# A product of the MLP backward pass, made in the output passes and reloaded from DRAM for the w2 gradient

## The chip, the cores and the metric

The kernel runs on one core of a Trainium2 chip. The core has a matrix engine (TensorE, PE in the profile, with its weight loads as PEld), a vector engine (VectorE, DVE), an engine for activations (ScalarE, ACT), a general-purpose engine (GpSimd, POOL) and a queue engine (SyncE, SP) that issues transfers. POOL issues transfers too, among them the gathers and scatters by index. Every engine works through its own list of instructions in order; semaphores make one wait for another. Sixteen DMA engines move the bytes of all queues. The metric is the device time of one execution in microseconds (us); less is better.

## What is computed

One block of a network, its output and the gradients of nine of its inputs, for 2048 tokens of width D = 1024 and an MLP of width F = 3584, in bf16. A row of modulation values (sa, ca, ga, sb, cb, gb) comes from a vector c. The forward pass, without its helpers:

```
mod = (silu(c) @ w_mod).reshape(1, 6, 1, -1)
sa, ca, ga, sb, cb, gb = (mod[:, k] for k in range(6))
h = layernorm(x) * (1 + ca) + sa
x = x + ga * A(h, w_r, w_i)
h = layernorm(x) * (1 + cb) + sb
x = x + gb * B(h, w1, b1, w2, b2)
...
out, vjp = jax.vjp(f, A_x, A_w_r, A_w_i, B_w1, B_b1, B_w2, B_b2, c, w_mod)
grads = vjp(grad_out)
```

A is a filter in the two-dimensional Fourier domain. B normalises its input, multiplies by w1, adds b1, applies gelu, multiplies by w2 and adds b2. The change concerns one intermediate of the backward pass, gB = grad_out * gb, a 2048 x 1024 array that is the gradient at the output of B. The gradient of w2 is the transposed hidden layer times gB.

## The kernel before

The tokens are cut into 16 groups of 128 (one per partition of the on-chip memory) and handled in four chunks of four groups, b = 0 to 3. A chunk doesn't hold four neighbouring groups: in it groups 0 and 3 are plain rows of the tensor, and groups 1 and 2 are rows in reversed order, an order that the Fourier stage wants. An input is therefore loaded into a chunk by `load_tok` (L126) with three transfers: one plain load on SP for groups 0 and 3 (L128), and two gathers by index on POOL (L131). `load_tok_half` (L135) does the same for one half h of the columns (L137 and L142); `store_tok_half` writes a chunk back with one plain store on SP (L155) and two scatters on POOL (L160). Intermediates that the kernel keeps in DRAM for itself (d_x1, d_n3, d_A and others) are stored in chunk order, so that one plain transfer moves a whole chunk (`chunk_rows`, L120).

The work goes through these stages, all in one program:

- the modulation rows, a product ph of grad_out * gb with the transposed w2 (L659), and the forward Fourier stage;
- the MLP stage, about 380 to 780 us of the span. It has 28 blocks (`z_block`, L762) that compute the hidden layer of one seventh of F for one chunk (L776) and its gelu and derivative on ScalarE and VectorE, and eight output passes (`bo_pass`, L803), one for each chunk b and column half h, here named (b,h). A pass multiplies the hidden layer by w2 in seven steps g = 0 to 6 (L817), each with a block of w2 loaded by SP into one of four slots (w2sA to w2sD, L812). After the seventh step it loads half a chunk of x1 into x1t (L822) and of grad_out into go (L823), copies the sums out of PSUM on ScalarE into bo (L826), forms go * bo, bo * gb and bo + x1t on VectorE (L827 to L829), and stores the result. Two steps into the next pass, TensorE sums the columns of go * bo in four matmuls `pa` (L836). The three parts bo, x1t and go belong to one tile, `otile`, of which there is one. A list `plan` (L853) fixes how blocks and steps follow one another; in pass (3,0) and (3,1) no blocks are left;
- the stage that multiplies by the transposed w1 (L996) and goes back through the second layer norm, chunk by chunk;
- the gradient of w2 (`gw2_mm`, L1089, matmuls at L1090). Before it, L1034 to L1041 make the four chunks of gB: `load_tok` from grad_out, then one multiply by the gb row on VectorE. The tiles gB0 to gB3 lie in the buffers px2 to px5, which until then hold the first four blocks of the transposed w1 (w1T). The hidden layer comes in through transposing loads on SP (`hh_load`, L1115), of which all but the first are issued after the last load of gB (L1174);
- the backward Fourier stage, in which pieces of the w2 and w1 gradients (`fill`) are laid between other work, and the w1 gradient (L1157).

The framework orders the instructions of each engine ahead of time by a priority, which is the place in the program unless `tc.high_priority()` raises it, and by a model of when each is ready; `tc.issue_after(x)` puts an instruction behind x on its engine. It inserts the waits on semaphores, also those of a buffer that is written while an earlier user still reads it. The order is thus not the program's: loads are often issued well ahead of their place in it.

Of the kernel before, what the change touches and what calls it, by code (L numbers as in the profile page):

```python
# [11 lines left out]
BF16 = mybir.dt.bfloat16  # L12
I32 = mybir.dt.int32
ACT = mybir.ActivationFunctionType
ALU = mybir.AluOpType
# [3 lines left out]
S = 2048  # L19
D = 1024  # L20
# [15 lines left out]
def kernel(  # L36
# [24 lines left out]
    nc = tc.nc  # L61
# [5 lines left out]
    dram = ctx.enter_context(tc.tile_pool(name="dram", bufs=1, space=bass.MemoryType.DRAM))  # L67
# [26 lines left out]
    opca_row, ga_row, opcb_row, gb_row = (rows4[:, r, :] for r in range(4))  # L94
# [9 lines left out]
    d_x1 = dram.tile([S, D], BF16, name="d_x1")  # L104
    d_A = dram.tile([S, D], BF16, name="d_A")
    d_n3 = dram.tile([S, D], BF16, name="d_n3")
    d_gx1 = dram.tile([S, D], BF16, name="d_gx1")
    d_ph = dram.tile([F, S], BF16, name="d_ph")
    d_hh = dram.tile([F, S], BF16, name="d_hh")
    d_gz = dram.tile([F, S], BF16, name="d_gz")  # L110
# [9 lines left out]
    def chunk_rows(dt, i):  # L120
        return dt[4 * i * P:4 * (i + 1) * P, :].rearrange("(q p) d -> p q d", p=P)

    def tok_flat(ap):
        return ap[0] if len(ap.shape) == 3 else ap

    def load_tok(t4, src, i, eng=None):  # L126
        s3 = tok_flat(src)
        ins = (eng or nc.sync).dma_start(out=t4[:, 0:4:3, :],  # L128
                          in_=bass.AP(tensor=s3.tensor, offset=s3.offset + 128 * i * D, ap=[[D, P], [1024 * D, 2], [1, D]]))
        for q in range(2):  # L130
            nc.gpsimd.indirect_dma_start(out=t4[:, 1 + q, :], out_offset=None, in_=s3,  # L131
                                         in_offset=bass.IndirectOffsetOnAxis(ap=xidx[:, 2 * i + q:2 * i + q + 1], axis=0))
        return ins

    def load_tok_half(t4, src, i, h):  # L135
        s3 = tok_flat(src)
        nc.sync.dma_start(out=t4[:, 0:4:3, :],  # L137
                          in_=bass.AP(tensor=s3.tensor, offset=s3.offset + 128 * i * D + h * KH, ap=[[D, P], [1024 * D, 2], [1, KH]]))
        s2 = s3.rearrange("n (h d) -> (n h) d", h=2)
        for q in range(2):  # L140
            k = 4 * i + 2 * q + h
            nc.gpsimd.indirect_dma_start(out=t4[:, 1 + q, :], out_offset=None, in_=s2,  # L142
                                         in_offset=bass.IndirectOffsetOnAxis(ap=oidx[:, k:k + 1], axis=0))
# [9 lines left out]
    def store_tok_half(dst, t4, i, h):  # L153
        s3 = tok_flat(dst)
        nc.sync.dma_start(out=bass.AP(tensor=s3.tensor, offset=s3.offset + 128 * i * D + h * KH, ap=[[D, P], [1024 * D, 2], [1, KH]]),  # L155
                          in_=t4[:, 0:4:3, :])
        s2 = s3.rearrange("n (h d) -> (n h) d", h=2)
        for q in range(2):
            k = 4 * i + 2 * q + h
            nc.gpsimd.indirect_dma_start(out=s2, out_offset=bass.IndirectOffsetOnAxis(ap=oidx[:, k:k + 1], axis=0),  # L160
                                         in_=t4[:, 1 + q, :], in_offset=None)
# [7 lines left out]
    def bcn(row, n):  # L169
        return bass.AP(tensor=row.tensor, offset=row.offset, ap=[row.ap[0], [0, n], row.ap[1]])  # L170

    def tt(out, a, b, op):
        return nc.vector.tensor_tensor(out=out, in0=a, in1=b, op=op)  # L173
# [476 lines left out]
    def ordered():  # L650
        return tc.issue_after(last_pe[0].ins)
# [93 lines left out]
    otile = []  # L745
# [57 lines left out]
    def bo_pass(b, h):  # L803
        cs_ = slice(h * KH, (h + 1) * KH)
        pbs = [(ps_f if b < NB - 1 or h == 0 else (ps_s, ps_d)[k % 2])("pbo") for k in range(4)]
        for i in range(4):
            with ordered():
                last_pe[0] = nc.tensor.matmul(pbs[i][:], lhsT=ones_bf[0:1, :], rhs=b2_row[0:1, cs_], start=True, stop=False)
        for g in range(7):
            wp = w2p[w2n[0] % 4]  # L810
            w2n[0] += 1
            nc.sync.dma_start(out=wp, in_=w2_v[:, g * 4:(g + 1) * 4, cs_])  # L812
            hh = hh_slots[(b * 7 + g) % 11]
            for i in range(4):
                for k in range(4):
                    with ordered():
                        last_pe[0] = nc.tensor.matmul(pbs[i][:], lhsT=hh[:, k, i * P:(i + 1) * P], rhs=wp[:, k, :],  # L817
                                                      start=False, stop=(g == 6 and k == 3))
            if g < 6:
                yield  # L820
        bo, x1t, go = (otile[0][:, k] for k in range(3))
        nc.sync.dma_start(out=x1t, in_=chunk_rows(d_x1, b)[:, :, cs_])  # L822
        load_tok_half(go, grad_out, b, h)  # L823
        for i in range(4):
            with tc.high_priority():
                last_ev[0] = nc.scalar.copy(out=bo[:, i, :], in_=pbs[i][:])  # L826
        tt(go, go, bo, ALU.mult)  # L827
        tt(bo, bo, bcn(gb_row[:, cs_], 4), ALU.mult)
        tt(bo, bo, x1t, ALU.add)  # L829
        store_tok_half(out_0, bo, b, h)  # L830

        yield
        pa = (ps_d if b < NB - 1 else ps_f)("pa")
        for i in range(4):
            with ordered():
                last_pe[0] = nc.tensor.matmul(pa[:], lhsT=ones_bf[:], rhs=go[:, i, :], start=(i == 0), stop=(i == 3))  # L836
        with tc.high_priority():
            if b == 0:
                nc.vector.tensor_copy(out=gacc[:, cs_], in_=pa[0:1, :])  # L839
            else:  # L840
                tt(gacc[:, cs_], gacc[:, cs_], pa[0:1, :], ALU.add)

    def bo_both(b):
        for h in range(2):
            late = bo_pass(b, h)
            for _ in range(7):
                next(late)
                yield
            bo_late.append(late)
# [116 lines left out]
    fold2_in = {}  # L966
# [67 lines left out]
    gBs = []  # L1034
    for b in range(NB):
        gb_t = reg.tile([P, 4, D], BF16, name=f"gB{b}", tag=PXT[2 + b])
        gb_in = load_tok(gb_t, grad_out, b)
        with tc.high_priority():
            with tc.issue_after(fold2_in[2].ins):
                tt(gb_t[:], gb_t[:], bcn(gb_row, 4), ALU.mult)  # L1040
        gBs.append(gb_t)  # L1041
    smA2 = reg.tile([P, 2, 4, 512], BF16, name="smA2", tag="sma")
    smB2 = reg.tile([P, 2, 4, 512], BF16, name="smB2", tag="smb")
# [213 lines left out]
```

## Time and profile before

| | us |
|---|---|
| runs: median (lowest, highest) of 3 | 1522.13 (1520.72, 1531.21) |
| span of the profiled execution | 1521.4 |
| VectorE multiplies of gB, 4 of 128x4096 | 2.29 each |
| VectorE multiplies of otile by a row, 8 of 128x2048 | 1.22 each |
| gathers of gB on POOL, 8: issue; to landing | 0.95 to 1.97; 10.3 to 13.2 |
| gathers of go on POOL, 16: issue; to landing (median) | 0.97 to 1.68; 5.0 |
| loads of x1t on SP, 8: to landing (median) | 5.7 |
| stores of d_gz on POOL, 28: issue; to landing (median, longest) | 0.75; 4.7; 9.9 |
| transposing loads hht on SP, 8: to landing (median) | 7.1 |

The profile is of one execution. Its span runs from the first to the last instruction; the times of the runs were measured without it. Times in views count from the start of the span. L173 is the line of the helper for element-wise operations, so those are told apart by their tiles; `rows` is the tile that holds the gb row.

### The profile page before, as it was taken

What the parts mean: (1) busy time and instruction counts of PE and PEld (TensorE: products, weight loads), DVE (VectorE), ACT (ScalarE), POOL (GpSimd) and SP (SyncE); (2) the same over time, 40 slices, a digit from 0 to 9 for tenths busy, and PEclk for the clock granted to TensorE, in tenths of its full rate; (3) what the DMA queues carried; (4) which work ended last, traced back from release to release, by engine and by line L of the source; (5) the groups of instructions that cost most, each with busy time, mean ns of one, the idle gap of its engine ahead of it and who ended that gap; (6) DMA issues with size and microseconds to landing.
All of it is one profiled execution on the core that took longest, in us unless ns stands there. A gap on an engine that the chain in (4) does not pass through costs nothing.

```text
span 1521.4 us, 18355 instructions
## 1 busy us (share of the span) xinstructions
PE 1437.8 (95%) x6831; PEld 667.6 (44%) x6831; DVE 1072.0 (70%) x1577; ACT 722.1 (47%) x956; POOL 363.5 (24%) x428
## 2 busy tenths in 40 slices
PE   5889899999999999999989999979998899999998
PEld 2434445444444444444334444434444444444443
DVE  5992868897799887877224977967066666898633
ACT  4765556668876666655012333322522344443211
POOL 5720621111112122220210101311033421322423
PEclk8999999999999999999999999989999999999999
DMA  9972745989587876999956336496288986766996
GB/s 327 282 207 66 198 150 176 280 258 339 193 265 238 211 254 216 257 282 271 322 170 205 135 101 221 109 275 176 63 201 225 235 242 183 197 174 163 257 206 195
DMA packets 358160, 324.27 MB, mean 213 GB/s; under 512 B 209187, under 2 KB 300849, under 8 KB 357816
## 3 DMA queue, kind: packets, MB, share of 16 engines
q1 hardware_dynamic: 324184, 207.71, 52.4%
q0 software_dynamic: 33888, 115.41, 22.5%
q8 instruction: 53, 0.87, 0.2%
q14 instruction: 35, 0.29, 0.1%
HBM read 164.15 MB, written 109.10 MB: 180 GB/s over the span
## 4 chain that ended last, share of the span: by engine, by line
PE 47%; DVE 22%; DMA 10%; issue 10%; ACT 6%; POOL 3%; SPq 1%; POOLq 0%; ACTq 0%; DVEq 0%
PE pbo L817 11%; PE pz L776 9%; PE gw2acc L1090 8%; PE pg L996 5%; DVE ct L173 4%; PE pv L544 3%; PE pu L451 3%; PE gw1acc L1157 2%; PE pp L659 2%; DVE got L895 2%; DVE fbuf L173 1%; DMA gB<-in_grad_out_dram 1%; DVE gn3a L900 1%; DMA out_dram<-otl 1%; DVE gt L173 1%
## 5 line engine op out<-in xcount | busy, mean ns | idle before, releaser
L659 PE MATMUL pp<-gBoT,wt 128*128 128x512 bf16 x896 | 200.4, 379 | 1.9 <-ACT pho L669 1.0
L1157 PE MATMUL gw1acc<-gzh,n3n 128*128 128x512 bf16 x896 | 197.0, 380 | 0.3 <-DMA gzh<-d_gz 0.3
L996 PE MATMUL pg<-w1T,gzr 128*128 128x512 bf16 x896 | 196.3, 380 | 0.4
L776 PEld LDWEIGHTS <-w 128*128 128x128 bf16 x896 | 87.7, 98 | 109.0 <-issue 3.8
L996 PEld LDWEIGHTS <-gzr 128*128 128x128 bf16 x896 | 88.0, 98 | 107.5 <-issue 2.9
L1157 PEld LDWEIGHTS <-n3n 128*128 128x128 bf16 x896 | 87.8, 98 | 104.3 <-issue 0.6
L659 PEld LDWEIGHTS <-wt 128*128 128x128 bf16 x896 | 87.4, 98 | 103.0 <-DMA wt<-in_B_w_dram 1.4
L776 PE MATMUL pz<-n3Tb,w 128*128 128x512 bf16 x448 | 99.1, 379 | 1.5 <-DVE w2sD L839 1.5
L1090 PE MATMUL gw2acc<-gB,hhsA 128*128 128x512 bf16 x448 | 100.1, 379 | 0.0
L776 PE MATMUL pz<-n3Ta,w 128*128 128x512 bf16 x448 | 98.7, 379 | 1.3 <-ACT gt L779 1.3
L817 PEld LDWEIGHTS <-hhA 128*128 128x128 bf16 x608 | 59.9, 99 | 79.0 <-issue 10.8
L1095 ACT CAST gwo<-gw2acc 128x512 bf16<-128x512 f32 x54 | 30.6, 584 | 122.4 <-PE gw2acc L1090 80.1
L779 ACT ACTIVATE gt<-pz,b_col 128x512 bf16<-128x512 f32 x112 | 72.9, 684 | 29.5 <-PE pz L776 29.0
L785 ACT ACTIVATE gt<-gt 128x2048 bf16<-128x2048 bf16 x28 | 53.4, 1910 | 64.4 <-DVE gt L173 64.4
L173 DVE TENSOR_TENSOR gt<-gt,gt 128x2048 bf16<-128x2048 bf16 x56 | 68.5, 1224 | 15.9 <-ACT gt L787 15.1
L1161 ACT CAST gwo<-gw1acc 128x512 bf16<-128x512 f32 x48 | 27.7, 584 | 109.1 <-PE gw1acc L1157 87.5
L173 DVE TENSOR_TENSOR ct<-ct 128x2048 bf16<-128x2048 bf16 x64 | 76.0, 1219 | 0.8
L1090 PE MATMUL gw2acc<-gB,hht 128*128 128x512 bf16 x256 | 58.9, 392 | 8.7 <-DVE gB L173 8.4
L1090 PEld LDWEIGHTS <-hhsA 128*128 128x128 bf16 x448 | 43.8, 98 | 50.4
L781 ACT ACTIVATE gt<-gt 128x2048 bf16<-128x2048 bf16 x28 | 53.5, 1910 | 7.6 <-DVE gb_acc L796 6.9
L787 ACT ACTIVATE gt<-gt 128x2048 bf16<-128x2048 bf16 x28 | 53.3, 1909 | 0.4
L1162 POOL DMA_DIRECT2D out_dram<-gwo x56 | 30.7, 551 | 77.9 <-ACT gwo L1161 38.3
(314 smaller groups left out, 2552.9 us busy)
## 6 DMA issues: line engine op xcount, KB each, us to landing
gzr<-d_gz SPq DMA_DIRECT2D x28, 512.0 KB, 7.7
wblk<-in_w_mod_dram SPq DMA_DIRECT2D x12, 1024.0 KB, 13.4
d_ph<-pho POOLq DMA_DIRECT2D x21, 512.0 KB, 5.2
out_dram<-otl POOLq DMA_DIRECT2D x40, 256.0 KB, 3.7
d_hh<-hhA POOLq DMA_DIRECT2D x19, 512.0 KB, 4.8
w2sD<-in_B_w_dram SPq DMA_DIRECT2D x14, 512.0 KB, 6.1
hhC<-d_ph SPq DMA_DIRECT2D x14, 512.0 KB, 5.1
w2sA<-d_ph SPq DMA_DIRECT2D x14, 512.0 KB, 4.0
```

The costliest lines, as they stand in the source:

```text
L173: return nc.vector.tensor_tensor(out=out, in0=a, in1=b, op=op)
L451: last_pu[0] = nc.tensor.matmul(pu[:], lhsT=fb[:, i, cl, c8 * P:(c8 + 1) * P], rhs=sm[:, i, :], start=(i == 0), stop=(i == 3))
L659: last_pe[0] = nc.tensor.matmul(pp[:], lhsT=wt[:, fg % 2, cch, k * P:(k + 1) * P], rhs=gBoT[j][:, cch, :], start=(cch == 0), stop=(cch == ...
L776: last_pe[0] = nc.tensor.matmul(pz[:], lhsT=w1s[g][:, cch, k * P:(k + 1) * P], rhs=n3T[:, cch, :], start=(cch == 0), stop=(cch == NDC - 1))
L779: nc.scalar.activation(out=zb[:, k, :], in_=pz[:], func=ACT.Identity, bias=b1_col[:, fc:fc + 1], scale=1.0)
L781: nc.scalar.activation(out=av, in_=zb, func=ACT.Square)
L785: nc.scalar.activation(out=sg, in_=bv, func=ACT.Sigmoid, scale=2.0 * GK)
L787: nc.scalar.activation(out=bv, in_=bv, func=ACT.Sigmoid, scale=-2.0 * GK)
L817: last_pe[0] = nc.tensor.matmul(pbs[i][:], lhsT=hh[:, k, i * P:(i + 1) * P], rhs=wp[:, k, :], start=False, stop=(g == 6 and k == 3))
L996: nc.tensor.matmul(pgs[i][:], lhsT=gzt[g][:, k, i * P:(i + 1) * P], rhs=w1Ts[g][:, k, h * KH:(h + 1) * KH], start=(g == 0 and k == 0), sto ...
L1090: nc.tensor.matmul(acc[:], lhsT=hh_s[hh_o[fc]][:, t, :], rhs=gBs[t // 4][:, t % 4, h * KH:(h + 1) * KH], start=(t == 0), stop=(t == NT - 1))
L1157: nc.tensor.matmul(acc[:], lhsT=n3ns[t // 4][:, t % 4, cch * P:(cch + 1) * P], rhs=gz2[t // 8][:, t % 8, :], start=(t == 0), stop=(t == NT ...
```

## The change

gB is made in the output passes. After step g = 2 of each pass the half chunk of grad_out is loaded into go, multiplied by the gb row into x1t, and x1t is stored by POOL to a new DRAM tensor d_gB in chunk order; then x1t is loaded from d_x1. Both loads stood after step 6 before. Ahead of the w2 gradient each gB tile is loaded from d_gB by one plain load on SP, without gathers and without a multiply.

```diff
+    d_gB = dram.tile([S, D], BF16, name="d_gB")
...
             for i in range(4):
                 for k in range(4):
                     with ordered():
                         last_pe[0] = nc.tensor.matmul(pbs[i][:], lhsT=hh[:, k, i * P:(i + 1) * P], rhs=wp[:, k, :],
                                                       start=False, stop=(g == 6 and k == 3))
+            if g == 2:
+                bo, x1t, go = (otile[0][:, k] for k in range(3))
+                load_tok_half(go, grad_out, b, h)
+                tt(x1t, go, bcn(gb_row[:, cs_], 4), ALU.mult)
+                nc.gpsimd.dma_start(out=chunk_rows(d_gB, b)[:, :, cs_], in_=x1t)
+                nc.sync.dma_start(out=x1t, in_=chunk_rows(d_x1, b)[:, :, cs_])
             if g < 6:
                 yield
-        bo, x1t, go = (otile[0][:, k] for k in range(3))
-        nc.sync.dma_start(out=x1t, in_=chunk_rows(d_x1, b)[:, :, cs_])
-        load_tok_half(go, grad_out, b, h)
...
     for b in range(NB):
         gb_t = reg.tile([P, 4, D], BF16, name=f"gB{b}", tag=PXT[2 + b])
-        gb_in = load_tok(gb_t, grad_out, b)
-        with tc.high_priority():
-            with tc.issue_after(fold2_in[2].ins):
-                tt(gb_t[:], gb_t[:], bcn(gb_row, 4), ALU.mult)
+        gb_in = nc.sync.dma_start(out=gb_t[:], in_=chunk_rows(d_gB, b))
         gBs.append(gb_t)
```

## The prediction

> **What bounds the kernel now.** The page's first part and its chain come first: TensorE is busy for 95% of the span and carries 47% of the chain, and one load of this change, gB from grad_out, stands in that chain by name.
>
> ```profile
> PE 1437.8 (95%) x6831; PEld 667.6 (44%) x6831; DVE 1072.0 (70%) x1577; ACT 722.1 (47%) x956; POOL 363.5 (24%) x428
> PE 47%; DVE 22%; DMA 10%; issue 10%; ACT 6%; POOL 3%; SPq 1%; POOLq 0%; ACTq 0%; DVEq 0%
> ```
>
> The timeline of TensorE shows where: the w2 gradient stutters at its start (start, duration, instruction, idle before it and who ended it).
>
> ```profile
> 997.21 1.02 PE L1090 MATMUL gw2acc<-gB,hht 128*128 128x512 bf16 x4 [0.25 <-issue]
> 999.38 1.02 PE L1090 MATMUL gw2acc<-gB,hht 128*128 128x512 bf16 x4 [1.16 <-DVE gB L173]
> 1005.50 1.87 PE L1090 MATMUL gw2acc<-gB,hht 128*128 128x512 bf16 x4 [5.09 <-DVE gB L173]
> 1009.52 20.29 PE L1090 MATMUL gw2acc<-gB,hht 128*128 128x512 bf16 x84 [2.15 <-DVE gB L173]
> ```
>
> The same stretch on VectorE: each multiply waits for a load, and the last two end their wait on SP's half of gB.
>
> ```profile
> 994.81 4.52 DVE L173 TENSOR_TENSOR gB<-gB,rows 128x4096 bf16<-128x4096 bf16 x2 [7.18 <-DMA gB<-in_grad_out_dram,xu]
> 1003.16 2.29 DVE L173 TENSOR_TENSOR gB<-gB,rows 128x4096 bf16<-128x4096 bf16 x1 [3.82 <-DMA gB<-in_grad_out_dram]
> 1007.18 2.29 DVE L173 TENSOR_TENSOR gB<-gB,rows 128x4096 bf16<-128x4096 bf16 x1 [1.73 <-DMA gB<-in_grad_out_dram]
> ```
>
> The windows (busy per engine with instructions, granted TensorE clock, DMA share, GB/s) say that the DMA engines are full there, and what the stutter costs.
>
> ```profile
> 990.00:995.00 5.00, 5.00 (x25) 2.25 (x23) 0.19 (x1) 0.60 (x2) 0.95 (x1) 1.00 0.98 362
> 995.00:1000.00 5.00, 3.60 (x17) 1.39 (x15) 4.33 (x2) 2.16 (x8) 2.98 (x1) 1.00 1.04 386
> 1000.00:1005.00 5.00, 0.41 (x2) 0.10 (x1) 1.84 (x1) 0.00 (x0) 0.55 (x1) 0.84 1.04 384
> 1005.00:1010.00 5.00, 2.34 (x6) 0.70 (x6) 3.27 (x3) 0.00 (x0) 0.00 (x0) 0.50 1.11 166
> 1010.00:1015.00 5.00, 5.00 (x17) 1.84 (x16) 3.93 (x12) 2.76 (x3) 0.00 (x0) 0.64 0.97 220
> ```
>
> From 995 to 1015 run 17+2+6+17 = 42 matmuls; at 0.216 us each (16 in 3.45 us on the chain) there is room for 92. So 50 x 0.216 = 10.9 us is all that can be won here.
>
> In the MLP stage (380 to 780) TensorE is busy 50.0 of 50 us in most windows. It waits for DMA only in pass (3,0), where no hidden blocks are left to cover it:
>
> ```profile
> 733.23 3.61 PE L817 MATMUL pbo<-w2sD,hhA 128*128 128x512 bf16 x16 [0.67 <-DMA w2sD<-in_B_w_dram]
> 747.19 5.30 PE L817 MATMUL pbo<-w2sC,hhA 128*128 128x512 bf16 x16 [1.92 <-DMA w2sC<-in_B_w_dram]
> ```
>
> **The change, part by part.** All sums go against this execution, 1521.4 us; the median of the runs, 1522.13, is 0.7 above it.
>
> *Out of the w2 stage: four multiplies, eight gathers.* The multiplies take 4 x 2.29 = 9.2 us of VectorE, but TensorE sees of them only what follows the last landing. gB3 reuses px5, and its load issues at 986.63, when the 48 matmuls that still follow w1T_3's last use (48 x 0.216 = 10.4 us before 996.96) begin: that gate stays. Its SP half landed at 1007.1 (the multiply's wait), its gathers (issued to 990.9, 10.3 us) by 1001.2. From 990 to 1005 the queues move 362 to 386 GB/s, and the change leaves the bytes of gB as they are (4 x 1 MB). I therefore let gB3 land at 1007.1 again and TensorE go on 0.1 later instead of at 1009.5: -2.4. The other end is that moving the gathers to SP clears the whole gap: -10.9.
>
> *Clock.* The rows above show 0.50 and 0.64 after the wait, and 17 matmuls in 5 us instead of 23 to 25. That loss, 8 x 0.216 = 1.7 us, is part of the 10.9; I keep it, since 1000 to 1007 stays nearly empty.
>
> *Reload on SP's queue.* SP issues four plain 1 MB loads where it had 0.5 MB. In place of the gathers, SP carries all the bytes, and behind it stand the transposed hh loads (hh1 to hh3, issued 995.38 to 1011.7, 5.4 us each). hh1 is needed after 4+16 matmuls, 4.3 us past gB3's landing, 1011.5; with SP free at 995.4 as now it lands at about 1000.8 + 7.1 (median) = 1008. Nothing added; the rival below has the other end.
>
> *Into the MLP stage: eight multiplies, 128x2048.* The same form takes 1.22 us there (otile rows), 9.8 us in all, on a VectorE that is busy 37 to 50 of each 50 us. The worst stretch, 420 to 470 (49.9 of 50), falls in pass (0,0), whose gather is issued at 374.9 and whose multiply fits in the gaps of 380 to 400 (5.1 and 6.3 of 10 us busy). hh for a block is made up to eleven slots ahead of its use, so I cost these at 0; with that cover gone it is 8 x 1.14 (start to start) = 9.1.
>
> *Into it: eight stores on POOL.* 0.75 us of issue each, like the d_gz stores. POOL is busy 10 of 50 us. If one waits for its multiply, the d_hh and d_gz stores and output scatters queue behind it; they release ph slots of blocks two ahead, so nothing reaches TensorE. The bytes do count: 0.52 MB each. Only where the DMA share is over 1 (passes (2,0), (2,1), (3,0), up to 373 GB/s) can they push w2 loads back, 1.4 us each; TensorE waits for such loads only in (3,0). Bounds 0 and 4.2; I take one, +1.4.
>
> *The moved loads.* The go load and its two gathers already issue just after the previous pass's pa matmuls (SP at 465.9 in a pass that ends at 518), so an earlier place in the program changes little. The x1 load does change: it now follows gather, multiply, POOL store and its landing. From the second gather's issue to x1 landed: 5.0 (gather, median) + 1.2 + 0.75 + 4.7 (d_gz landing) + 5.7 (x1 landing) = 17.4 us. Passes (0,1) to (2,1) then have x1 at 494.7, 558.6, 598.8, 648.7, 699.8, against adds at 521.9, 567.6, 618.7, 665.7, 719.3: hidden by 9 us or more. In (3,0) the gather is at 736.0, x1 lands at 753.4, the add was at 750.8; with the 9.9 us that the slowest d_gz store took it is 758.6. The output store at 752.13 then goes 2.6 to 7.8 later, and behind it on SP stand the loads of w2sC (752.62) and w2sD. w2sC is needed at 763.55 and lands in 4.7 to 8.6: a wait of 0 to 5.5. I take 2.3, the late store (760.4 + 0.8) with the fast landing of the emptier queue after 750. In (3,1) x1 lands at 776.8, before the add at 780.7, and go x bo, which pa waits for, stands ahead of that add. Sum: -2.4 + 1.4 + 2.3 = +1.3.
>
> **The rivals.**
> *A, the whole gap closes* (0.14). For it: POOL takes 0.95 to 1.97 us a gather, and SP's halves of gB2 and gB3 took 19.7 and 20.4 us; one plain load could be quicker. Against: the full DMA windows. 1521.4 - 10.9 + 0.7 = 1511.2.
> *B, SP becomes the queue that is late in the w2 stage* (0.10). SP's issue of the gB3 half took 8.70 us; doubled, SP is free at 1004.1, hh1 issued by 1009.5 and landed 4.7 to 7.1 later, 1014.2 to 1016.6, against 1011.5: waits of 2.7 to 5.1 in place of part of the gain, 1525.8 to 1528.2 with the MLP terms. The Trainium skill (DMA: Bandwidth & Descriptors, Queues, rings and completion order) has each DMA engine take turns, packet by packet, between the queues that have work; by it the gathers lose a turn of their own, all of gB stands in SP's line behind au and n3u, and the sum would be +4.0 to +6.4 instead of +1.3. The trace agrees in that POOL's parts of gB2 and gB3 landed before SP's parts, which had been issued earlier.
> *C, slower: x1 blocks SP in the last passes* (0.20). SP works in order. If the x1 load of (3,0) stands ahead of the w2sD load issued at 740.19, SP is held until the d_gB store lands, 753.7; w2sD, needed at 752.33, comes 4.7 to 9.6 later: 6.1 to 11.0 lost. In (3,1), ahead of the last w2 load (760.29, needed 770.46), 4.6 to 9.8. Both: 1534 to 1544. It decides only if the order puts x1 before those loads; 4 slots of w2 hide it elsewhere. For it: SP already waits on L155 for VectorE 36.8 us in 6 times.
> *D, the multiply isn't hidden, only moved* (0.06): 9.1 more, 1532.5.
>
> **How the numbers follow.** My forecast (0.50) is 1521.4 + 1.3 + 0.7 = 1523; its own range is 1518 (MLP terms at 0, part of A) to 1529 (their upper ends). A reaches down to 1511, C up to 1534 for half its weight; so 1511 to 1536 leaves out the upper half of C and tails. One per cent is 15 us, about what a measurement can tell here (the runs lie between 1520.7 and 1531.2). Faster by over 1% (below 1507) needs more than the gap holds: 0.03. Slower by over 1% (above 1537) is half of C and a tail, 0.12. Within: 0.85.
>
> **What would show it.** In the changed profile: no VectorE multiply on gB; TensorE's first L1090 groups still broken, released by DMA d_gB, running on from about 1007 less any earlier shift (A: no break, clock 1.00; B: breaks named hht); pass (3,0)'s w2s waits a few us longer than 3.0 (C: over 9, with SP's x1 load waiting for DMA d_gB). It would be wrong if TensorE waited in passes (0,0) to (2,1), or if gB3 landed well before 1005.

## The result, and the profile after

The changed kernel takes 1560.83 us (median of 6 runs, 1556.77 to 1563.04) beside 1524.78 us (6 runs, 1520.72 to 1533.04) of the kernel before on the same chip: ratio 1.0234, 95% interval [1.0212, 1.0255]. It is slower by 36 us, and the forecast of 1523 and its range, 1511 to 1536, are wrong. The ratios here and below leave out one slowed execution, of stores_only (3050.43 us). The profiled execution has a span of 1559.2 us, 37.8 more than before.

From each trace the same marks were read: the first matmul of the pz blocks, the first and last pg matmul (L996 before, L1000 after), the first matmul of gw2acc on an hhsA tile (the ninth row block of the w2 gradient), the first of gw1acc.

| stretch, us | before | after | difference |
|---|---|---|---|
| start to first pz | 346.2 | 347.0 | +0.8 |
| first pz to first pg (the MLP stage) | 433.6 | 465.9 | +32.3 |
| first to last pg | 216.8 | 217.6 | +0.8 |
| last pg to first hhsA (the start of the w2 gradient) | 101.3 | 97.4 | -3.9 |
| hhsA to first gw1acc | 201.5 | 206.0 | +4.5 |
| from there to the end | 222.1 | 225.4 | +3.3 |

The start of the w2 gradient, which the change was to shorten, became shorter, by more than the 2.4 us of the forecast. The loss is in the MLP stage, where the eight multiplies went.

The engine totals and the chain by engine (first and fourth part of the page) of the changed kernel: the work of VectorE is as before (1072.0 then), and PE's part of the chain fell from 47 to 30%. PE's busy time can't be compared, since fewer of its records are in this trace.

```profile
PE 1442.4 (93%) x6697; PEld 670.2 (43%) x6831; DVE 1072.5 (69%) x1582; ACT 718.5 (46%) x955; POOL 355.4 (23%) x428
...
PE 30%; DVE 10%; DMA 6%; issue 4%; ACT 3%; SPq 1%; POOL 1%; POOLq 0%; ACTq 0%; DVEq 0%
```

The start of the w2 gradient in the timeline of TensorE, after. There were three broken-off groups that waited for the multiply of gB; now there is one wait, for the first tile of the hidden layer.

```profile
1013.85 17.00 PE L1000 MATMUL pg<-w1T,gzr 128*128 128x512 bf16 x77
1036.23 4.02 PE L1091 MATMUL gw2acc<-gB,hht 128*128 128x512 bf16 x9 [5.38 <-DMA hht<-d_hh]
```

SP's timeline of the changed kernel says why: the transposing load of that tile, which SP issued at 974.61 between the loads of gB before, stands behind all four of them.

```profile
1020.52 1.22 SPq L1041 DMA_DIRECT2D gB<-d_gB  x1
1021.79 19.08 SPq L1116 DMA_TRANSPOSE hht<-d_hh  x4
```

The windows of the MLP stage, after (columns as in the prediction). TensorE was busy for 50.0, 50.0 and 43.2 of these 50 us before, at clocks of 1.00, 1.00 and 0.95. VectorE is busy for less time than before in the first two (42.3 and 39.8 then): it is not overloaded.

```profile
530.00:580.00 50.00, 44.73 (x195) 19.53 (x198) 36.61 (x52) 27.47 (x28) 10.15 (x12) 0.98 0.71 232
...
630.00:680.00 50.00, 42.37 (x181) 18.37 (x184) 37.53 (x55) 25.78 (x24) 10.94 (x12) 0.93 0.88 233
...
730.00:780.00 50.00, 42.05 (x175) 17.61 (x177) 26.94 (x38) 15.81 (x17) 7.88 (x9) 0.90 1.01 305
```

The costliest groups have the cause in one line: sixteen multiplies of otile by a row (eight of them new), each of 1224 ns as before, but with 55.6 us of idle time ahead of them.

```profile
L174 DVE TENSOR_TENSOR otile<-otile,rows 128x2048 bf16<-128x2048 bf16 x16 | 19.6, 1224 | 55.6 <-DMA otile<-in_grad_out_dram,xu 55.5
```

The list of waits (us in total, times, longest) has what follows from it. The first line is ScalarE's wait for VectorE in the gelu chain, which was 64.4 in 24 before, with a longest of 5.6; the second did not exist.

```profile
ACT gt L786 <- DVE gt L174: 119.6, 24, 12.7
...
DVE otile L174 <- DMA otile<-in_grad_out_dram,xu: 55.5, 8, 13.3
```

One of the eight, in pass (1,0), followed from engine to engine through the timelines of the changed kernel. POOL issues the gathers of go (L143) behind the output scatters of the pass before (L161), where they stood in the kernel before too:

```profile
540.42 1.02 POOL L161 DMA_INDIRECT out_dram<-otile,xu  x1 [9.09 <-ACT gt L786]
544.83 1.00 POOL L161 DMA_INDIRECT out_dram<-otile,xu  x1 [3.38 <-ACT gt L780]
...
546.94 1.01 POOL L143 DMA_INDIRECT otile<-in_grad_out_dram,xu  x1 [0.30 <-issue]
548.26 0.96 POOL L143 DMA_INDIRECT otile<-in_grad_out_dram,xu  x1 [0.30 <-issue]
```

VectorE has reached the product at 543.6, 7.62 us before it can start and before POOL has issued the gathers, and the multiplies of the gelu chain (`gt`) stand behind it:

```profile
551.22 1.23 DVE L174 TENSOR_TENSOR otile<-otile,rows 128x2048 bf16<-128x2048 bf16 x1 [7.62 <-DMA otile<-in_grad_out_dram,xu]
552.36 1.22 DVE L174 TENSOR_TENSOR gt<-gt,hhA 128x2048 bf16<-128x2048 bf16 x1
```

ScalarE waits for that chain, and copies the sums of the pass (L830) two blocks later:

```profile
559.31 1.91 ACT L786 ACTIVATE gt<-gt 128x2048 bf16<-128x2048 bf16 x1 [12.71 <-DVE gt L174]
...
571.41 1.91 ACT L786 ACTIVATE gt<-gt 128x2048 bf16<-128x2048 bf16 x1 [4.00 <-DVE gt L174]
573.35 1.91 ACT L788 ACTIVATE gt<-gt 128x2048 bf16<-128x2048 bf16 x1
575.17 2.03 ACT L830 CAST otile<-pbo 128x512 bf16<-128x512 f32 x4
```

And TensorE, which needs the PSUM banks of these sums for the next pass, stops:

```profile
575.79 1.83 PE L809 MATMUL pbo<-b_row,ones_bf 1*128 1x512 bf16 x4 [2.87 <-ACT otile L830]
577.55 3.17 PE L818 MATMUL pbo<-w2sC,hhA 128*128 128x512 bf16 x7
```

The windows there add a second loss: after the stop the granted clock (the third figure from the end) falls to a half for some 3 us, and only seven matmuls fit into 3.17 us.

```profile
575.00:576.00 1.00, 0.21 (x1) 0.09 (x1) 0.70 (x1) 1.00 (x3) 0.63 (x1) 1.00 1.09 336
576.00:578.00 2.00, 1.65 (x6) 0.36 (x5) 1.93 (x3) 2.00 (x5) 0.00 (x0) 0.89 0.92 281
578.00:580.00 2.00, 2.00 (x6) 0.71 (x5) 2.00 (x2) 1.97 (x4) 0.00 (x0) 0.50 0.86 248
```

Over 380 to 820 TensorE's waits of more than 0.2 us for another engine or a transfer add up to 33.1 us in 14 places, against 11.5 in 9 before: 21.6 more. The clock below 1.00 in the windows of 50 us from 480, and 20 at the end, makes up for 16.4 us (each window times what its clock lacks), against 4.8 before: at most 11.6 more, since a low clock in idle time costs nothing. Together that is about the loss of the stage.

Not all of these waits end on ScalarE. Of the 33.1 us, 10.7 end on ScalarE's copies of the sums (2.1 before) and 10.2 on two loads of w2 into w2sD, in passes (2,0) and (3,1). The first of these two, in the timeline of TensorE:

```profile
671.63 1.46 PE L818 MATMUL pbo<-w2sC,hhA 128*128 128x512 bf16 x5
678.47 6.02 PE L818 MATMUL pbo<-w2sD,hhA 128*128 128x512 bf16 x16 [5.38 <-DMA w2sD<-in_B_w_dram]
```

That load stands on SP behind the load of x1t (L825), for which SP was held 11.7 us until the d_gB store had landed; the other is held in the same way, for 10.5 us, until 777.19. This is rival C's mechanism:

```profile
665.41 0.37 SPq L825 DMA_DIRECT2D otile<-d_x  x1
665.83 3.71 SPq L953 DMA_TRANSPOSE w1T<-in_B_w_dram  x2
671.72 0.37 SPq L771 DMA_DIRECT2D w2sA<-d_ph  x1
672.19 1.08 SPq L813 DMA_DIRECT2D w2sD<-in_B_w_dram  x1
```

### The profile page after: what moved, and what is told of

It reads as the page before. It is cut to its first block, busy times and chain, and to the rows that moved or that the text cites. A ratio compares the mean times of both kernels' runs of the same rounds, so it can differ in the third digit from the quotient of the medians.

```text
span 1559.2 us, 18215 instructions
## 1 busy us (share of the span) xinstructions
PE 1442.4 (93%) x6697; PEld 670.2 (43%) x6831; DVE 1072.5 (69%) x1582; ACT 718.5 (46%) x955; POOL 355.4 (23%) x428
## 4 chain that ended last, share of the span: by engine, by line
PE 30%; DVE 10%; DMA 6%; issue 4%; ACT 3%; SPq 1%; POOL 1%; POOLq 0%; ACTq 0%; DVEq 0%
PE gw1acc L1158 9%; PE gw2acc L1091 9%; PE pg L1000 5%; DVE got L899 2%; PE pu L452 2%; PE pv L545 2%; DVE gn3a L904 1%; DMA hht<-d_hh 1%; PE po L610 1%; ACT got L903 1%; DVE gt L174 1%; PE pcs L485 1%; DVE gn3b L904 1%; DVE ct L174 1%; DVE gn3a L1021 1%
## 5 line engine op out<-in xcount | busy, mean ns | idle before, releaser
L1000 PE MATMUL pg<-w1T,gzr 128*128 128x512 bf16 x884 | 196.5, 381 | 1.1 <-ACT gn3a L1005 0.2
L1000 PEld LDWEIGHTS <-gzr 128*128 128x128 bf16 x896 | 88.0, 98 | 107.9 <-issue 3.5
L777 PE MATMUL pz<-n3Ta,w 128*128 128x512 bf16 x440 | 98.5, 379 | 4.2 <-DVE w2sD L843 1.8
L780 ACT ACTIVATE gt<-pz,b_col 128x512 bf16<-128x512 f32 x112 | 70.8, 684 | 11.7 <-PE pz L777 9.4
L174 DVE TENSOR_TENSOR otile<-otile,rows 128x2048 bf16<-128x2048 bf16 x16 | 19.6, 1224 | 55.6 <-DMA otile<-in_grad_out_dram,xu 55.5
```

The costliest lines, as they stand in the source:

```text
L777: last_pe[0] = nc.tensor.matmul(pz[:], lhsT=w1s[g][:, cch, k * P:(k + 1) * P], rhs=n3T[:, cch, :], start=(cch == 0), stop=(cch == NDC - 1))
L780: nc.scalar.activation(out=zb[:, k, :], in_=pz[:], func=ACT.Identity, bias=b1_col[:, fc:fc + 1], scale=1.0)
L1000: nc.tensor.matmul(pgs[i][:], lhsT=gzt[g][:, k, i * P:(i + 1) * P], rhs=w1Ts[g][:, k, h * KH:(h + 1) * KH], start=(g == 0 and k == 0), sto ...
```

## The experiments

The theory after this reading, D in a sharper form: it is the wait of VectorE for the gather, not the 1.2 us of work, that costs the time. Its rivals were: SP held by the new store (L825, the load of x1t, waits for the d_gB store 68.2 us in 8 times; rival C); the bytes of the stores; and the earlier place of the loads. First an overview, with the kernel before on the same chip as 1; the mark is the first pg matmul (779.8 before, 812.9 after) in one profile each.

| kernel | ratio, 95% interval | first pg |
|---|---|---|
| own_buffer | 1.0250 [1.0210, 1.0291] | 812.9 |
| pinned | 1.0076 [1.0049, 1.0104] | 788.4 |
| late_product | 1.0047 [1.0024, 1.0071] | 787.3 |
| w2_stage_only | 0.9946 [0.9926, 0.9965] | 777.8 |
| tiny_wait | 1.0248 [1.0208, 1.0287] | 818.1 |
| own_pinned | 1.0037 [1.0013, 1.0061] | 791.4 |
| own_pinned_hh | 1.0062 [1.0038, 1.0086] | 793.0 |
| w2_stage_hh | 0.9982 [0.9952, 1.0011] | 777.6 |
| stores_only | 1.0053 [1.0026, 1.0080] | 783.0 |
| loads_only | 0.9994 [0.9969, 1.0020] | 777.5 |
| scale_psum | 0.9988 [0.9966, 1.0010] | 778.8 |
| scale_sbuf | 0.9973 [0.9954, 0.9992] | 778.2 |

**own_buffer**: the product gets a tile of its own, so x1t no longer waits for the store.

```diff
+        otile.append(reg.tile([P, 4, BW], BF16, name="gprod", tag="sb")[:])
...
-                tt(x1t, go, bcn(gb_row[:, cs_], 4), ALU.mult)
-                nc.gpsimd.dma_start(out=chunk_rows(d_gB, b)[:, :, cs_], in_=x1t)
                 nc.sync.dma_start(out=x1t, in_=chunk_rows(d_x1, b)[:, :, cs_])
+                load_tok_half(go, grad_out, b, h)
+                tt(otile[1], go, bcn(gb_row[:, cs_], 4), ALU.mult)
+                nc.gpsimd.dma_start(out=chunk_rows(d_gB, b)[:, :, cs_], in_=otile[1])
```

> The changed kernel, but the product has a tile of its own, so x1t is loaded where no store holds it and SP is never held by a d_gB store; the multiply still stands early on VectorE. Theory D (VectorE stands at the multiply, waiting for the gather, and the gelu steps behind it come late): VectorE's waits on the gather stay near 55 us in 8 passes and the time stays at 1550 to 1562. Theory S (SP stands at the x1 load, and the ph and w2 loads behind it come late): 1520 to 1532. Theory B (the added bytes and instructions as such): about 1555.

1560.06 us, no better than the change itself. SP waits for the d_gB store only once more (9.2 us, ahead of a load for a later stage), but VectorE's wait for the gather is still there, in all eight passes:

```profile
DVE gprod L174 <- DMA otile<-in_grad_out_dram,xu: 59.1, 8, 13.0
```

TensorE's waits for w2sD shrink from 10.2 to 0.4 us, but those of the hidden blocks for ScalarE's gelus (`pz` behind `gt`) grow from 4.4 to 11.7, and the sum of its waits stays at 32.4. As long as VectorE waits, a free SP wins nothing.

**pinned**: the changed kernel, with the multiply put behind the last VectorE step of the block before it.

```diff
-            tt(av, av, sg, ALU.add)
+            last_z[0] = tt(av, av, sg, ALU.add)
...
-                tt(x1t, go, bcn(gb_row[:, cs_], 4), ALU.mult)
+                with tc.issue_after(last_z[0].ins):
+                    tt(x1t, go, bcn(gb_row[:, cs_], 4), ALU.mult)
```

> The changed kernel, but the multiply is put behind the last VectorE step of the block before it, by which time the gather should have landed; x1t is still loaded behind multiply and d_gB store. Theory D: VectorE's waits on the gather fall below 15 us outside passes (3,0) and (3,1), and the time falls to 1522 to 1538. Theory S: SP is held as long or longer, 1556 to 1570. Theory B: about 1560, no change.

1534.97 us: about two thirds of the loss is gone, while SP is still held by the store for 51.8 us in 6 times. In the trace more than VectorE's order has changed: the d_gB stores on POOL and the loads of x1t on SP, which wait for the multiply, also come later in their lists. So this run alone doesn't tell D from C; tiny_wait below does. The gather is waited for in the two last passes only, where no blocks are left to put in between:

```profile
DVE otile L174 <- DMA otile<-in_grad_out_dram,xu: 20.4, 2, 16.7
```

**late_product**: the loads stay after step 6; go * bo goes to the own tile, and go * gb is made in place after the sum of the pass, and stored.

```diff
-        tt(go, go, bo, ALU.mult)
+        tt(otile[1], go, bo, ALU.mult)
...
+        tt(go, go, bcn(gb_row[:, cs_], 4), ALU.mult)
+        nc.gpsimd.dma_start(out=chunk_rows(d_gB, b)[:, :, cs_], in_=go)
```

> Product tile and late multiply together: go*bo goes into a tile of its own, and go*gb is made in place after the output sum, so nothing on VectorE waits for a gather and nothing on SP for a d_gB store ahead of x1t. Multiplies, stores, bytes and the plain reload are those of the change. Theories D and S both: the MLP stage ends at 780 to 784 as in the kernel before, the w2 stage keeps the 3.9 us that it won, so 1516 to 1524. Theory B: 1545 or more.

1531.8 us, above the 1516 to 1524 expected of both theories. VectorE waits for no gather any more, and still 0.5% is left; TensorE's longest new wait is 5.73 us for a block of w2 (w2sA) just behind the stretch where the DMA engines are fullest (a share of 1.12 from 680 to 730 in the kernel before).

**w2_stage_only**: the kernel before with a plain load of grad_out into gB. The rows that need reversing and the product with gb are left out.

```diff
-        gb_in = load_tok(gb_t, grad_out, b)
-        with tc.high_priority():
-            with tc.issue_after(fold2_in[2].ins):
-                tt(gb_t[:], gb_t[:], bcn(gb_row, 4), ALU.mult)
+        gb_in = nc.sync.dma_start(out=gb_t[:], in_=chunk_rows(tok_flat(grad_out), b))
```

> The kernel before with only the w2 stage's part of the change: gB tiles are loaded plainly, from grad_out itself, without gather, order and the product with gb, which this run leaves out. If the plain reload wins what the changed trace shows from the end of the w1 stage to the first matmul after the forward transform (100.9 to 97.1 us), the time is 1517 to 1522 against 1522 to 1525; if the 4.6 us lost in the Fourier stage and the 2.8 at the very end come from the reload too, it is 1524 to 1530.

1516.25 us. This is the prize of the change without its price: 0.5%, just below the expected 1517 to 1522. The timeline of TensorE shows the same single wait as the changed kernel:

```profile
1001.66 23.35 PE L1087 MATMUL gw2acc<-gB,hht 128*128 128x512 bf16 x96 [5.83 <-DMA hht<-d_hh]
```

**tiny_wait**: the kernel before, with the loads where the change has them and one copy of 128x16 elements of go on VectorE, into a tile that nobody reads. No product, no store, no reload.

```diff
+            if g == 2:
+                bo, x1t, go = (otile[0][:, k] for k in range(3))
+                nc.sync.dma_start(out=x1t, in_=chunk_rows(d_x1, b)[:, :, cs_])
+                load_tok_half(go, grad_out, b, h)
+                nc.vector.tensor_copy(out=otile[1], in_=go[:, 1:3, 0:8])
```

> The kernel before, w2 stage and all, with one thing added in each output pass: after step 2 the two loads are placed as in the change and VectorE copies 16 columns per partition of go's gathered groups into a small tile that nobody reads. No product, no store, no reload, x1t loaded freely. The copy does next to no work but must wait for the gather in VectorE's order. Theory D: VectorE waits some 40 to 60 us for the gather in the eight passes and the time is 1540 to 1558 against 1522 to 1526. If what cost the time is the multiply's work, the stores, or SP: 1520 to 1528.

1564.82 us beside 1528.41, more than the 1540 to 1558 expected; VectorE waits 67.7 us for the gather. Eight copies of 0.17 us, 1.4 us in all, cost as much as the whole change. Two of them in the timeline of VectorE:

```profile
488.74 0.17 DVE L824 COPY tiny<-otile 128x16 bf16<-128x16 bf16 x1 [6.98 <-DMA otile<-in_grad_out_dram,xu]
...
557.89 0.17 DVE L824 COPY tiny<-otile 128x16 bf16<-128x16 bf16 x1 [8.19 <-DMA otile<-in_grad_out_dram,xu]
```

**loads_only** is tiny_wait without that copy (and its tile): only the place of the loads in the program is changed.

```diff
-                nc.vector.tensor_copy(out=otile[1], in_=go[:, 1:3, 0:8])
```

> tiny_wait without the tiny copy: the loads of x1t and go stand after step 2 of each pass, and nothing on VectorE reads go there; no product, no store, no reload. It asks whether tiny_wait lost its 2.5% to the wait of VectorE or to the place of the loads. Theory (the wait is the loss): VectorE waits nowhere for go in mid-pass, first pg matmul within 4 us of 779.8, ratio 0.997 to 1.005. Rival (the earlier loads collide with those of w2 and are the loss): first pg matmul beyond 800, ratio 1.015 or more.

1525.93 us beside 1526.07. The earlier place in the program costs nothing, and moves little: in the MLP stage POOL's list is that of the kernel before, and on SP three loads change places with a neighbour. The gathers of pass (0,1) go out at 476.4 and 478.5 as in the kernel before (475.2, 477.3). ScalarE's wait in the gelu chain is that of the kernel before:

```profile
ACT gt L785 <- DVE gt L173: 63.9, 23, 5.6
```

tiny_wait and loads_only differ by one tiny copy in each pass, and by 2.5%. It is not that the framework ordered the rest in another way: in the MLP stage of the two traces ScalarE and POOL go through the same instructions in the same order, VectorE does but for the eight copies, and SP's lists differ in the place of one load.

**own_pinned** joins own_buffer and the pin of pinned.

```diff
-                tt(otile[1], go, bcn(gb_row[:, cs_], 4), ALU.mult)
+                with tc.issue_after(last_z[0].ins):
+                    tt(otile[1], go, bcn(gb_row[:, cs_], 4), ALU.mult)
```

> Product tile of its own (x1t is loaded freely, go is free after pa) and the multiply behind the block's last VectorE step. By theory D with a small share of S, the MLP stage ends within 4 us of the kernel before (779.8) and the 7.7 us that the plain reload won alone remain in good part: 1516 to 1524. If the 8 stores and their 4.2 MB cost by themselves what late_product still lost (16 us), 1528 to 1534.

1535.12 us beside 1528.41. The pin takes the ratio from 1.0250 in own_buffer to 1.0037; in neither kernel does the load of x1t wait for a store (the d_gB stores move with the multiply). Yet the expected 1516 to 1524 and an end of the MLP stage within 4 us of 779.8 were both missed (791.4 here), and the time is just above the 1528 to 1534 that it gave for stores that cost: VectorE still waits for the gather 30.3 us in 3 of the last passes, and a small loss stays, as in late_product.

**stores_only** asks for that rest: the kernel before, and at the end of each pass a store of half a chunk that is not read again.

```diff
         store_tok_half(out_0, bo, b, h)
+        nc.gpsimd.dma_start(out=chunk_rows(d_gB, b)[:, :, cs_], in_=bo)
```

> The kernel before with one thing more: at the end of each output pass POOL also stores the half chunk of bo (its 0.52 MB are never read again) to d_gB. No early loads, no product, no reload; the w2 stage stays as it is in the kernel before. It asks what is left of the loss when no wait is added, as in late_product (ratio 1.0047) and own_pinned (1.0037), although the plain reload alone gained (0.9946). Theory bytes (the eight stores take the place of w2 and w1T loads in the crowded stretch and hold POOL's scatters back): MLP stage 5 to 10 us longer, first pg matmul at 784 to 790 instead of 779.8, time 1528 to 1536 beside 1522 to 1528 of the kernel before, ratio 1.003 to 1.007. Rival (the stores are free, and what is left is the multiplies or the order that the reload gives to the later loads): first pg matmul within 2 us of 779.8, ratio 0.998 to 1.002.

1534.15 us beside 1526.07. The stores alone cost 0.5%, what w2_stage_only gained. TensorE now waits for w2 loads in passes (3,0) and (3,1) in its timeline, where the longest such wait was 1.92 before:

```profile
730.51 5.30 PE L818 MATMUL pbo<-w2sA,hhB 128*128 128x512 bf16 x16 [4.57 <-DMA w2sA<-in_B_w_dram]
...
752.13 3.62 PE L818 MATMUL pbo<-w2sC,hhA 128*128 128x512 bf16 x15 [1.54 <-DMA w2sC<-in_B_w_dram]
```

The MLP stage ends 3.2 us later for it, less than the 5 to 10 expected; where the rest of the 8 us arises the profile doesn't say.

**own_pinned_hh** is own_pinned with the loads of gB behind the first transposing load of the hidden layer, **w2_stage_hh** is w2_stage_only with the same (and with the same part left out). They ask whether that load's place on SP is what still limits the start of the w2 gradient.

```diff
-    for b in range(NB):
-        gb_t = reg.tile([P, 4, D], BF16, name=f"gB{b}", tag=PXT[2 + b])
-        gb_in = nc.sync.dma_start(out=gb_t[:], in_=chunk_rows(d_gB, b))
-        gBs.append(gb_t)
...
     next(todo)
+    for b in range(NB):
+        gb_t = reg.tile([P, 4, D], BF16, name=f"gB{b}", tag=PXT[2 + b])
+        gb_in = nc.sync.dma_start(out=gb_t[:], in_=chunk_rows(d_gB, b))
+        gBs.append(gb_t)
```

> own_pinned with the first transposing load of the hidden layer issued ahead of the gB loads instead of behind them. In the changed trace TensorE waited 5.4 us for that load at the start of the w2 gradient. If it is only its place on SP, the wait goes and the time is 3 to 6 us below own_pinned; if the DMA engines are full anyway and gB lands later by as much, no difference.

> w2_stage_only (plain reload of grad_out, without order and product) with the hidden layer's first load ahead of the gB loads: 1510 to 1514 if the 5.8 us wait for that load goes, 1516 if gB lands later instead.

The gain did not come, which was the second branch of both expectations: 1537.36 us (ratio 1.0062) and 1522.16 us (0.9982). The wait for hht is gone in own_pinned_hh (gw2acc starts at 1011.2, right behind the last pg matmul), but TensorE now waits for gB:

```profile
1011.19 1.89 PE L1090 MATMUL gw2acc<-gB,hht 128*128 128x512 bf16 x8
1017.80 1.87 PE L1090 MATMUL gw2acc<-gB,hht 128*128 128x512 bf16 x4 [4.72 <-DMA gB<-d_gB]
1020.44 3.57 PE L1090 MATMUL gw2acc<-gB,hht 128*128 128x512 bf16 x8 [0.78 <-DMA gB<-d_gB]
```

Last pg to first hhsA is 98.5 (96.8 in own_pinned), and 98.7 in w2_stage_hh (97.6 in w2_stage_only), where the waits for gB are 6.28 and 0.70. With the DMA engines full (413, 390 and 387 GB/s from 1015 to 1030 in the changed kernel), one load's gain is another's delay.

**scale_psum** and **scale_sbuf** are another way to the same end: the gb row scales the columns of the w2 gradient, so it can be multiplied into the result. Both gather plain grad_out into gB; the first multiplies as a result leaves PSUM, the second in place in on-chip memory. The second:

```diff
-        with tc.high_priority():
-            with tc.issue_after(fold2_in[2].ins):
-                tt(gb_t[:], gb_t[:], bcn(gb_row, 4), ALU.mult)
...
         if h == 1:
+            tt(gwo[:, fc % 2], gwo[:, fc % 2], gb_row, ALU.mult)
             nc.gpsimd.dma_start(out=out_6[fc * P:(fc + 1) * P, :], in_=gwo[:, fc % 2])
```

In scale_psum the copy itself becomes the product:

```diff
-            nc.any.tensor_copy(out=gwo[:, fc % 2, h * KH:(h + 1) * KH], in_=acc[:])
+            tt(gwo[:, fc % 2, h * KH:(h + 1) * KH], acc[:], gb_row[:, h * KH:(h + 1) * KH], ALU.mult)
```

> A version for the same end without a wait in the MLP stage: the kernel before, with grad_out itself gathered into gB, no multiply of gB, and the gb row multiplied into each result of the w2 gradient as it leaves PSUM (56 products of 128x512 on VectorE in place of ScalarE's copies; the row scales the columns of the result). The MLP stage stays as in the kernel before: first pg matmul within 2 us of 779.8, no wait of VectorE for a gather. The w2 stage: TensorE waits for gB's landing and no longer for the multiply, 2 to 5 us less between the last pg and the first hhsA matmul (101.3 before). The 56 products, estimated at 0.7 us each from the 0.68 us of VectorE's copies of gw1acc, add 39 us to a VectorE that also carries the backward Fourier stage: theory hidden, ratio 0.996 to 0.999; rival, VectorE late in the Fourier stage: hhsA to gw1acc longer than 201.4 by 5 to 20, ratio 1.001 to 1.012.

> As scale_psum, but ScalarE copies the results out of PSUM as before and VectorE multiplies each 128x1024 row block of gwo in place before POOL stores it: 28 products, estimated at 0.6 us each (a quarter of the 2.29 us of a 128x4096 product), 16 us where the kernel before had 9.2 us of multiplies of gB in the same stage. Theory hidden: 2 to 5 us less between the last pg and the first hhsA matmul, nothing added behind it, ratio 0.996 to 0.999. Rival (the products hold the two halves of gwo longer, and the stores and the next copies come late): hhsA to gw1acc longer than 201.4 by 3 or more, ratio 1.000 to 1.005.

1521.02 us (no difference shown) and 1521.18 us beside 1524.65: scale_sbuf is faster than the kernel before by 0.3%, and the one version of this study that is so while it computes the whole reference. TensorE's timeline in it: the breaks are shorter than before and end on the landing of gB, no longer on a multiply.

```profile
995.08 1.89 PE L1087 MATMUL gw2acc<-gB,hht 128*128 128x512 bf16 x8
1000.12 1.02 PE L1087 MATMUL gw2acc<-gB,hht 128*128 128x512 bf16 x4 [3.15 <-DMA gB<-in_grad_out_dram]
1004.13 20.38 PE L1087 MATMUL gw2acc<-gB,hht 128*128 128x512 bf16 x84 [2.98 <-DMA gB<-in_grad_out_dram]
```

The 28 products are 19.1 us of work where 9.2 were before, and TensorE waits 2.7 us in 2 times for an instruction on gwo, which it did not before. The groups of VectorE name a wait of the products' own, for ScalarE's copies:

```profile
L173 DVE TENSOR_TENSOR gwo<-gwo,rows 128x1024 bf16<-128x1024 bf16 x28 | 19.1, 687 | 19.7 <-ACT gwo L1092 19.6
```

In single profiles, last pg to first hhsA is 98.5 in scale_sbuf and 96.3 in scale_psum (101.3 before). The next stretch, to the first gw1acc, is 206.5 in scale_sbuf, the mark of that run's rival, though the time is the theory's. In scale_psum it is 193.0, but the last stretch is 230.1, 8.0 more than before.

## Why the prediction was wrong

- **The step that failed** is "Into the MLP stage: eight multiplies", priced at 0, with 9.1 "with that cover gone". Both ends count work: 8 x 1.14. What the change put into VectorE's list was also a wait for a gather, and the working compared the gather's issue with the gaps of VectorE for pass (0,0) only. For the others the figures stood in the next part but one, where x1's landing was counted from the second gather: 494.7 in pass (0,1) less 17.4 is an issue at 477.3, and a landing 5.0 later. At what time VectorE would come to the multiply was never asked. Measured: 55.5 us of waiting in front of 9.8 us of work, and 32 us more in the MLP stage. tiny_wait beside loads_only shows that it is the wait, and own_pinned beside own_buffer that a later place on VectorE takes most of it away. The prediction's own sign of being wrong, TensorE waiting in passes (0,0) to (2,1), came true: 2.75 us in (0,1), 2.87 between (1,0) and (1,1), 5.38 in (2,0).
- **The cover** that was named, hidden blocks made up to eleven slots ahead, was real but does not cover this: ScalarE's copies of the sums stand in the same queue as the gelus (the episode of pass (1,0) above), and TensorE needs the PSUM banks, not only the blocks.
- **Rival D** had the right place and, counting work and not the wait, the wrong price: 9.1 for about 32. It had a chance of 0.06.
- **Rival C** came true as a wait (68.2 us of SP in 8 times), and 10.2 us of TensorE's waits stand behind it, in (2,0) and (3,1). It set the time no more than that: own_buffer took both away and gained nothing, since the waits behind ScalarE's gelus grew instead. (With VectorE's wait shortened, own_pinned stands beside pinned at 1.0037 to 1.0076; their intervals overlap.) The added 2.3 us for w2sC can't be told from the rest.
- **The w2 stage** was right in sign, -2.4 forecast and -3.9 measured, but by another way, so that the nearness of the two numbers is in part luck. As forecast, the gap did not close. What ends it is no longer gB: when gB landed the trace doesn't show, since nothing waited for it. The wait moved to hht and is 5.38 us long, which is rival B's mechanism and near its 2.7 to 5.1; the loss of 4.0 to 6.4 that B made of it did not come. That the bytes are the limit fits the two hh experiments, where the wait went back to gB.
- **The stores**: forecast +1.4 within 0 to 4.2. stores_only puts them at 0.5% (interval 0.3 to 0.8), some 8 us of which 3.2 lie in the MLP stage; the term was too small, and the plain reload gains no more than they cost.
- **Left open**: the 4.5 us between hhsA and gw1acc and the 3.3 us behind them. The first stretch takes 205.6 in stores_only and 211.2 in loads_only, whose work there is that of the kernel before (201.5), so a single profile doesn't settle it. Why the stores cost more than they delay the MLP stage is open too. Also open is what late_product still loses: the plain reload alone (0.9946) and the stores alone (1.0053) make 0.9999 together, it measured 1.0047, and the rest is little more than the intervals allow.
- **Slips in the working** that change none of this: 50 x 0.216 is 10.8; the times of rival B come to +3.7 to +6.1, not +4.0 to +6.4; C's 753.7 comes to 752.9 from the terms of the moved loads (736.0 + 5.0 + 1.2 + 0.75 + 9.9); and the wait at 747.19 is at the first step of pass (3,1), not in (3,0).

How such a wait hides in a profile: a duration tells nothing of it. The new multiplies take 1224 ns a piece, as the old ones did; the 55.6 us stand in the idle column. The Trainium skill (Perfetto Trace Analysis, Per-instruction lifecycle: what the profiler-reported window actually captures) says so in general: the time in which an instruction waits for its semaphores lies outside of its recorded slice. The trace agrees.

## What to carry to other kernels

An instruction that is moved onto an in-order engine is priced by when its input lands, and not by its duration alone: put the landing time beside the moment at which the engine gets there, for every pass, and look at who stands behind it. If the landing is late, pin the instruction behind work that covers it, or move the product to a place where its operand has long been there; a scale by column can be taken out of an operand and put on the result. And a store and a reload that only save a gather have to earn their bytes where the DMA engines are already full.

## What the runs showed that was not expected

- Eight copies of 0.17 us made a kernel of 1528 us slower by 2.5% (tiny_wait), because a chain of three engines runs through the queue that they stop.
- A stop of TensorE costs more than its length. After a wait of 2.75 us for ScalarE the matmuls went on at once, and the granted clock fell between 1 and 2 us later: 0.61, 0.50, 0.50 and 0.69 in the four windows of 1 us from 492, then 1.00 again. 31 matmuls took 8.84 us, where 32 take 7.07 at the full clock.

```profile
490.95 8.84 PE L777 MATMUL pz<-n3Tb,w 128*128 128x512 bf16 x31 [2.75 <-ACT gt L780]
```

Likewise the sixteen matmuls after the wait of 5.38 us took 6.02 us instead of 3.62. The Trainium skill (TensorE: Matmul & The Clock Gate, What's actually happening) has the clock halved after an idle window of about 3.4 us that runs free of the kernel. The half clock here agrees, but the stop of 2.75 us, as this profile reckons it, is shorter than that window and was enough.
